# A second mixture's VectorE, ScalarE and transfers in a hand-written order, and an earlier reload of x

## The chip, the cores and the metric

One core of one Trainium2 chip runs the kernel. The metric is the device time of one execution in microseconds; lower is better.

## The reference

Packed attention feeds a mixture of four experts (the first mixture), whose output feeds a second block with a tanh-shrink (called the second mixture here):

```python
p_packed = sm_attn(p, k, v)                  # B=4, H=8, S=576, D=64, 32 packed rows
x = sm_attn(q, p_packed, p_packed)           # -> x, 2304 x 512
for e in range(4):                           # first mixture, 512 -> 1024 -> 512
    out += prob[:, e:e+1] * (np.maximum(x @ w1[e], 0.0) @ w2[e])
h = out @ w_in                               # second mixture, 512 -> 2048
g = h - np.tanh(h)
result = g @ w_out                           # 2048 -> 512
```

All is float32.

## The kernel before

TensorE multiplies float32 in two parts, a high part that its fast format holds and the rest as a low part, and three products (high x high, high x low, low x high) stand for one. ScalarE writes the high part, VectorE subtracts it for the low part.

**First mixture.** Its last chunk ends with the products of L629 (w2) and those of L579. Its results are stored in DRAM and loaded again (`reload`, L643 to L650, one DMA of 256 KB for each 128 tokens, tile `x2`, name x in the trace) for the second mixture; `x_quad` (L685 on) transposes the first six of them on TensorE (L696, tile xps). The order of this part is a list of tokens, one list for each turn: `LASTA` and `LAST` are the last two, `l06` is the reload of tiles 0 to 5, and `q0` to `q3` are `x_quad`. SyncE issues all DMAs, in the order of these lists.

**Second mixture.** The tokens go in NU = 3 units of 768, the 2048 columns in NG = 8 groups of 256: 24 blocks n, block n being group n % 8 of unit n // 8. A block's 768 x 512 by 512 x 256 is done as seven products of quarter size, whose operands are four quarters of x (B11 to B22; B12 only enters differences) and four differences of them (T1 to T4). Each is six matmuls of 128x384 (L795) into one of two PSUM banks (tile h3ps, called X and Z here). The bank is copied out or summed into h: `keep` is a copy on ScalarE (L804), `add` a sum on VectorE (L808), and there are four copies k0 to k3 and three sums a0 to a2 for a block. Products, copies and sums of one block go X0 k0 Z0 a0, X1 k1 Z1 k2, X2 a1 Z2 a2, X3 k3.

The elementwise work on a block is done for its two halves A and B (`elem`, L974, with L985 to L994). h - tanh(h) is taken from tanh where |h| is large and from a polynomial where it is small, so one half is five ScalarE and five VectorE operations on 128x768: ScalarE makes z (square, L985), the mask gh (L986), y in two steps (L987, L988) and t (tanh, L989), VectorE y from z (L990), t (h - tanh, L991), h (L992, L993) and the choice by the mask (L994, `copy_predicated`). `elem_split` then writes the high part (L1006, ScalarE, gh) and the low part (L1012, VectorE, gl). `s4` (L1029) multiplies g by w_out in six tiles of 128 tokens and two halves (ff 0 and 1), three matmuls of 128x512 each, and sums over the unit's eight groups in six PSUM banks (ops). After a unit's last group `s4` evacuates the banks, by turns on VectorE (L1041) and ScalarE (L1039), and stores them.

TensorE's order is written out by hand (`manual_schedule`). In slot n it is X0 Z0, four tiles of block n-2 in ff 0, X1 Z1, four more (two of each ff), X2 Z2, two, X3, two. In slots n = 1 and 9, 10 the next unit's x is transposed too (`x_raw`, L734, tile xps from the pool of six banks), and in slots 3 to 7 and 11 to 15 `x_prep` makes the differences and the parts of it, one step in each slot.

VectorE, ScalarE and SyncE are ordered by the scheduler here, by its own times, with `high_priority(offset=PRIO)` on the copies, sums, transposes' copies and evacuations, and `issue_after` that ties `x_prep` to the sums and copies of block n-1. Weights come by DMA: `load_g` (L771, tile wg, 1.8 MB for a block) and `load_o` (wo, two of 512 KB).

Names of the tables below: h3ps, ops and xps are PSUM banks, gh, gl high and low parts, xr a transposed quarter of x, po an evacuated output tile.

Of the kernel before, what the change touches and what calls it, by code (L numbers as in the profile page):

```python
# [27 lines left out]
PREP = (0, 3, 11)  # L28

# [29 lines left out]
    "d614 _ g7100 _ d615 _ g7101 _ d616 _ g7102 _ d617 g7103 _ d618 "  # L59
# [8 lines left out]
    "w0 l06 g7110 _ d710 _ q0 g7111 _ d711 _ g7112 _ q1 d712 g7113 q2 d713 q3 d714 l69 s0 d715 s1 d716 s2 d717 s3 d718 "  # L68
# [4 lines left out]
def kernel(  # L73
# [647 lines left out]

    def x_raw(u, q, k):
# [21 lines left out]
    def x_prep(u, k):  # L744

        if k == 0:
            x_tiles(u)
            x_split(u, "B11")
            xr["T1"] = xr["B11"]
            x_minus("T1", "B12", "B11")  # L750
        elif k == 1:
            x_split(u, "T1")
            x_split(u, "B22")
        elif k == 2:
            xr["T2"], xr["T3"] = xr["T1"], xr["B12"]
            x_minus("T2", "B22", "T1")
            x_minus("T3", "B22", "B12")
            x_split(u, "T2")
        elif k == 3:
            x_split(u, "B21")  # L760
            xr["T4"] = xr["B22"]
            x_minus("T4", "B21", "T2")
        else:
            x_split(u, "T4")
            x_split(u, "T3")

    wg, xz, hs, late_h, summed, copied = {}, {}, {}, {}, {}, {}
# [5 lines left out]
    def s3(n, step):  # L773


        x = xc[n // NG]
        if step == 0:
            if n == 0:
                xz[n] = [
                    pl.tile([128, 2, 512], F32, tag=tg, name="h3ps")[:, 0, 0:HT]  # L780
                    for pl, tg in ((ps2, "p2"), (psw[0], "pw"))
                ]
                hs[n] = [[u2t([128, HT], F32, "h3") for _ in range(2)] for _ in range(2)]
            else:
                xz[n] = [late["xz"].tile([128, 512], F32, tag="xz", name="h3ps")[:, 0:HT] for _ in range(2)]
                t = late_h[n] = [late["hh"].tile([128, 2, HT], F32, tag="hh", name="h3") for _ in range(2)]
                hs[n] = [[t[k][:, 0], t[k][:, 1]] for k in range(2)]
        X, Z = xz[n]
        (c11, c12), (c21, c22) = hs[n]

        def mul(ps, slot, c, start, stop):
            k = 0
            for kk in range(2):
                for a, b in ((0, 0), (0, 1), (1, 0)):
                    nc.tensor.matmul(  # L795
                        out=ps, lhsT=wg[n][:, a, slot, 128 * kk:128 * kk + 128],
                        rhs=x[c][b][kk] if isinstance(x[c][b], list) else x[c][b][:, kk],
                        start=(start and k == 0), stop=(stop and k == 5), skip_group_check=True,
                    )
                    k += 1  # L800

        def keep(t, ps):
            with tc.high_priority(offset=PRIO):
                copied[n] = nc.scalar.activation(out=t, in_=ps, func=ACTF.Copy).ins  # L804

        def add(t, ps):
            with tc.high_priority(offset=PRIO):
                summed[n] = nc.vector.tensor_tensor(out=t, in0=ps, in1=t, op=ALU.add).ins  # L808

        if step == 0:  # L810
            mul(X, 0, "B11", True, False)
            keep(c11, X)
            mul(Z, 1, "B21", True, True)
            add(c11, Z)
        elif step == 1:
            mul(X, 4, "T2", False, False)
            keep(c12, X)
            mul(Z, 3, "T1", True, False)
            keep(c22, Z)
        elif step == 2:  # L820
            mul(X, 5, "T3", False, False)
            add(c22, X)
            mul(Z, 6, "B22", False, True)
            add(c12, Z)
        else:
            mul(X, 2, "T4", False, True)
            keep(c21, X)
# [146 lines left out]
    def elem(n, fb):  # L974
# [3 lines left out]
        h = hs[n][fb]  # L978
        if n:
            parts = [(slice(None), late_h[n][fb])]  # L980
        else:
            parts = [(k, h[k]) for k in range(2)]
        for k, hk in parts:
            zk, tk, yk, mk = (x if isinstance(k, slice) else x[:, k] for x in (z, t, y, hi))
# [11 lines left out]
    def elem_split(n, fb):  # L996
# [3 lines left out]
        if n:  # L1000
            g = late_h[n][fb].rearrange("p a b -> p (a b)")
            parts = [(0, 2 * HT, g)]
        else:
            parts = [(HT * k, HT * k + HT, hs[n][fb][k]) for k in range(2)]
        for a, b, g in parts:
            nc.scalar.activation(out=hi[:, a:b], in_=g, func=ACTF.Copy)  # L1006
# [9 lines left out]

    ops = {}

    def s4(n, ts, ff):
        u, i = divmod(n, NG)  # L1020
        for t in ts:
# [12 lines left out]
            if i == NG - 1 and ff == 1:  # L1034
                r0 = 768 * u + 128 * t
                o = u2t([128, 512], F32, "po")
                with tc.high_priority(offset=PRIO):
                    if t % 2:
                        nc.scalar.activation(out=o, in_=ps, func=ACTF.Copy)  # L1039
                    else:  # L1040
                        nc.vector.tensor_copy(out=o, in_=ps)  # L1041
                nc.sync.dma_start(out=out[r0:r0 + 128, :], in_=o)
# [4 lines left out]
    for n in range(1, N2 + 2):  # L1047
        if n + 1 < N2:
            load_g(n + 1)
        if n - 1 < N2:  # L1050
            load_o(n - 1)
        order = [[("s", n, k)] if n < N2 else [] for k in range(4)]
        m = n - 2
        if m >= 0:
            order[0].append(("o", m, range(0, 4), 0))
            order[1] += [("o", m, range(4, 6), 0), ("o", m, range(0, 2), 1)]
            order[2].append(("o", m, range(2, 4), 1))
            order[3].append(("o", m, range(4, 6), 1))
# [74 lines left out]
```

## Time and profile before

| | us |
|---|---|
| median of three runs | 1095.16 (1094.71 to 1099.7) |
| profiled execution, its own time | 1096.69 |
| span of its trace | 1094.8 |
| mean granted clock of TensorE | 0.994 |
| TensorE busy | 1068.6 (98%) |
| VectorE, ScalarE busy | 870.3, 619.7 |
| second mixture, X0 of block 2 to X0 of block 24 | 717.07 to 1072.32 |

The span goes from the first to the last instruction. Since TensorE is busy nearly throughout, its own timeline, with the idle time before an instruction and what ended it in square brackets, is the view to read; the queues of the others are read where it waits.

### The profile page before, as it was taken

What the parts mean: (1) busy time and instruction counts of PE and PEld (TensorE: products, weight loads), DVE (VectorE), ACT (ScalarE), POOL (GpSimd) and SP (SyncE); (2) the same over time, 40 slices, a digit from 0 to 9 for tenths busy, and PEclk for the clock granted to TensorE, in tenths of its full rate; (3) what the DMA queues carried; (4) which work ended last, traced back from release to release, by engine and by line L of the source; (5) the groups of instructions that cost most, each with busy time, mean ns of one, the idle gap of its engine ahead of it and who ended that gap; (6) DMA issues with size and microseconds to landing.
All of it is one profiled execution on the core that took longest, in us unless ns stands there. A gap on an engine that the chain in (4) does not pass through costs nothing.

```text
span 1094.8 us, 16535 instructions
## 1 busy us (share of the span) xinstructions
PE 1068.6 (98%) x6356; PEld 904.2 (83%) x6356; DVE 870.3 (79%) x1331; ACT 619.7 (57%) x987; POOL 198.9 (18%) x153
## 2 busy tenths in 40 slices
PE   8899999999999999999999998999999999999998
PEld 6677887888788788888888887888888888989886
DVE  4667879988889775798889864879988888888876
ACT  3345454555554446445454432677786777777674
POOL 0100225544535102243324210000000000000000
PEclk9899999999999999999999999999999999999999
DMA  9616446547436653554364404454555554556432
GB/s 351 209 29 252 154 155 220 182 140 280 175 118 213 241 174 102 178 202 165 118 229 148 169 39 144 161 221 148 202 193 170 205 186 156 206 196 217 174 134 87
DMA packets 57582, 192.74 MB, mean 176 GB/s; under 512 B 6432, under 2 KB 8480, under 8 KB 54432
## 3 DMA queue, kind: packets, MB, share of 16 engines
q1 hardware_dynamic: 57504, 191.69, 50.1%
q8 instruction: 50, 0.82, 0.3%
q14 instruction: 28, 0.23, 0.1%
HBM read 144.74 MB, written 46.92 MB: 175 GB/s over the span
## 4 chain that ended last, share of the span: by engine, by line
PE 78%; DVE 11%; ACT 7%; issue 2%; DMA 1%; POOL 0%; SPq 0%; DVEq 0%; ACTq 0%
PE yps L629 31%; PE ops L1029 13%; PE h3ps L795 12%; PE hpx L579 7%; PE hpz L579 6%; PE wps L484 3%; PE hps L531 2%; PE pv L256 1%; ACT z L985 1%; ACT t L989 1%; DVE h L994 1%; DVE h L993 1%; ACT gh L986 1%; DVE y L990 1%; DMA x<-xs 1%
## 5 line engine op out<-in xcount | busy, mean ns | idle before, releaser
L1029 PE MATMUL ops<-wo,gh 128*128 128x512 f32 x576 | 179.0, 392 | 0.7 <-ACT gh L1006 0.7
L640 DVE SCALAR_TENSOR_TENSOR x<-yps,pn,x 128x512 f32<-128x512 f32 x126 | 93.9, 745 | 47.9 <-PE yps L629 47.7
L1029 PEld LDWEIGHTS ops<-wo,gh 128*128 128x128 f32 x576 | 106.7, 188 | 19.4 <-ACT gh L1006 1.1
L629 PE MATMUL yps<-w2h,h0h 128*128 128x512 f32 x288 | 117.5, 408 | 2.6 <-DVE a2l L324 1.4
L1029 PE MATMUL ops<-wo,gl 128*128 128x512 f32 x288 | 113.7, 395 | 0.9 <-DVE gl L1012 0.9
L629 PE MATMUL yps<-w2h,h0l 128*128 128x512 f32 x288 | 113.6, 394 | 0.0
L629 PE MATMUL yps<-w2h,h1h 128*128 128x512 f32 x288 | 113.2, 393 | 0.0
L629 PE MATMUL yps<-w2l,h0h 128*128 128x512 f32 x288 | 113.0, 392 | 0.0
L629 PE MATMUL yps<-w2h,h1l 128*128 128x512 f32 x288 | 112.6, 391 | 0.0
L629 PE MATMUL yps<-w2l,h1h 128*128 128x512 f32 x288 | 112.5, 391 | 0.0
L795 PE MATMUL h3ps<-xh,wg 128*128 128x384 f32 x384 | 107.4, 339 | 1.8 <-ACT h L804 1.6
L629 PEld LDWEIGHTS yps<-w2h,h0h 128*128 128x128 f32 x288 | 54.1, 188 | 34.5 <-issue 21.8
L579 PE MATMUL hpx<-th,wp 128*128 128x288 f32 x336 | 81.8, 299 | 0.6 <-ACT p L586 0.5
L1006 ACT ACTIVATE gh<-h 128x768 fp32r<-128x768 f32 (+1 forms) x50 | 41.0, 819 | 67.5 <-DVE h L994 67.5
L377 POOL TENSOR_TENSOR fo<-fo,f 128x512 f32<-128x512 f32 x32 | 44.0, 1377 | 179.2 <-DVE f L373 97.7
L795 PEld LDWEIGHTS h3ps<-xh,wg 128*128 128x128 f32 x384 | 70.3, 188 | 6.0 <-ACT h L804 3.7
L471 POOL TENSOR_TENSOR w2l<-wraw,w2h 128x512 fp32r<-128x512 f32 x32 | 43.1, 1368 | 147.4 <-ACT w2h L469 145.6
L991 DVE TENSOR_TENSOR t<-h,t 128x768 f32<-128x768 f32 (+1 forms) x50 | 46.1, 923 | 26.4 <-ACT t L989 26.4
L795 PE MATMUL h3ps<-xl,wg 128*128 128x384 f32 x192 | 64.6, 337 | 0.2 <-DVE xl L150 0.2
L795 PE MATMUL h3ps<-xbh,wg 128*128 128x384 f32 x224 | 63.2, 339 | 1.6 <-ACT h L804 1.1
L1029 PEld LDWEIGHTS ops<-wo,gl 128*128 128x128 f32 x288 | 54.0, 187 | 12.8 <-DVE gl L1012 1.3
L629 PEld LDWEIGHTS yps<-w2l,h1h 128*128 128x128 f32 x288 | 54.4, 189 | 12.1
(177 smaller groups left out, 2634.7 us busy)
## 6 DMA issues: line engine op xcount, KB each, us to landing
wg<-wing SPq DMA_DIRECT2D x24, 1792.0 KB, 7.4
wraw<-in_w_dram SPq DMA_DIRECT2D x48, 512.0 KB, 5.6
wo<-wout SPq DMA_DIRECT2D x48, 512.0 KB, 5.4
w2s<-w2h SPq DMA_DIRECT2D x16, 512.0 KB, 7.1
w2s<-w2l SPq DMA_DIRECT2D x16, 512.0 KB, 7.4
f<-in_win_dram SPq DMA_DIRECT2D x16, 512.0 KB, 7.1
f<-in_wout_dram SPq DMA_DIRECT2D x16, 512.0 KB, 6.6
wing<-f SPq DMA_DIRECT2D x32, 256.0 KB, 4.3
```

The source lines that it names most:

```text
L256: nc.tensor.matmul(out=pv[64 * h:64 * h + 64, jj, :], lhsT=kv_v[b][c][0:n, 128 * j + 64 * h:128 * j + 64 * h + 64], rhs=a1t[:, c, k0:k0 + ...
L377: nc.gpsimd.tensor_tensor(out=lf, in0=lf, in1=st[:, :, 1].bitcast(F32), op=ALU.mult)
L471: nc.gpsimd.tensor_tensor(out=l[:, k], in0=r[:, k], in1=f(h[:, k]), op=ALU.subtract)
L484: nc.tensor.matmul(out=ps[32 * j:32 * j + 32, r, :], lhsT=ppbd[p][d, bi, j, 32 * r:32 * r + 32], rhs=raw[0, c, j // 2][d, j % 2, :],)
L531: nc.tensor.matmul(out=ps[:, ff, 0:n], lhsT=a[c, p, bi][:, g, c0:c0 + 128], rhs=x[p][:, g, t0:t0 + n], start=(k == 0), stop=(k == 5),)
L579: nc.tensor.matmul(out=ps[:, ff, 0:HB], lhsT=W[a][:, slot, c0], rhs=x[b], start=(start and k == 0), stop=(stop and k == 2), skip_group_che ...
L629: nc.tensor.matmul(out=ps, lhsT=a[:, ff, o:o + 128], rhs=w[c, fp][:, ff], start=(k == 0), stop=(k == 11),)
L640: last[0] = nc.vector.scalar_tensor_tensor(out=x2[tt], in0=ps, scalar=pn[:, tt, e:e + 1], in1=x2[tt], op0=ALU.mult, op1=ALU.add,).ins
L795: nc.tensor.matmul(out=ps, lhsT=wg[n][:, a, slot, 128 * kk:128 * kk + 128], rhs=x[c][b][kk] if isinstance(x[c][b], list) else x[c][b][:, k ...
L991: nc.vector.tensor_tensor(out=tk, in0=hk, in1=tk, op=ALU.subtract)
L1006: nc.scalar.activation(out=hi[:, a:b], in_=g, func=ACTF.Copy)
L1029: nc.tensor.matmul(out=ps, lhsT=a, rhs=wo[n][ff][:, w], start=(i == 0 and ff == 0 and k == 0), stop=(i == NG - 1 and ff == 1 and k == 2), ...
```

## The change

It does four things.

- The token `l06` moves from the start of `LAST` to the end of `LASTA`, ahead of the weight load of the first block in SyncE's queue.
- Slots n = 2 to 25 are put under `manual_schedule` for SyncE, VectorE and ScalarE as well. One line for each kind of slot says the order: X and Z are products, k and a copies and sums, o tiles of `s4`, v evacuations, R and C transposes and their copies, P, H and D the parts of `x_prep`; a letter with A or B is one elementwise operation on that half (z, t, y, q, m, g on ScalarE, d, c, r, f, p, l on VectorE, l the low part).
- Elementwise work on block n-1 stands in slot n, its last low part in slot n+1, and the tiles of `s4` are those of block n-2 as before.
- Banks X and Z change places from block to block (`xz[n].reverse()`), and of the six copies of x in slot 10 one moves from VectorE to ScalarE.

```diff
+SLOT = (
+    "lB zA tA X0 k0 dA yA Z0 a0 cA P o030 qA mA rA fA zB pA X1 tB k1 dB Z1 k2 cB yB o450 o011 qB rB gA X2 a1 fB mB "
+    "Z2 a2 H pB o231 lA D X3 k3 gB o451 "
+)
...
+SLOT_LAST = (
+    "lB zA tA yA dA cA qA mA rA fA o030 pA zB tB gA lA o450 o011 dB yB cB qB mB rB o231 fB pB o451 gB nB "
+)
+SLOT_OUT = "o050 o001 v0 o111 v1 o221 v2 o331 v3 o441 v4 o551 v5 "
...
 LASTA = (
-    "d614 _ g7100 _ d615 _ g7101 _ d616 _ g7102 _ d617 g7103 _ d618 "
+    "d614 _ g7100 _ d615 _ g7101 _ d616 _ g7102 l06 _ d617 g7103 _ d618 "
 )
...
 LAST = (
-    "w0 l06 g7110 _ d710 _ q0 g7111 _ d711 _ g7112 _ q1 d712 g7113 q2 d713 q3 d714 l69 s0 d715 s1 d716 s2 d717 s3 d718 "
+    "w0 g7110 _ d710 _ q0 g7111 _ d711 _ g7112 _ q1 d712 g7113 q2 d713 q3 d714 l69 s0 d715 s1 d716 s2 d717 s3 d718 "
 )
...
-            if u == 2 and (k == 1 or q == 3):
+            if u == 2 and k == 1:
                 nc.vector.tensor_copy(out=o, in_=ps)
...
+    X_PREP = (
+        ("", "hB11", "lB11 sT1"),
+        ("", "hT1 hB22", "lT1 lB22"),
+        ("sT2 sT3", "hT2 hB21", "lT2"),
+        ("lB21 sT4", "hT4 hT3", ""),
+        ("lT4 lT3", "", ""),
+    )
...
+            if n % 2 == 0:
+                xz[n].reverse()
...
-        for u in (1, 2):
-            if 0 <= n - PREP[u] < 5:
-                with tc.issue_after(summed[n - 1]), tc.issue_after(copied[n - 1]):
-                    x_prep(u, n - PREP[u])
...
+    progs = {
+        NG + 1: SLOT_RAW, NG + 2: SLOT_RAW2, 2 * NG + 1: SLOT_END, 2 * NG + 2: "v5 v4 " + SLOT,
+        N2: SLOT_LAST, N2 + 1: SLOT_OUT,
+    }
+    with tc.manual_schedule(engines=rest):
+        for n in range(2, N2 + 2):
+            slot(n, progs.get(n, SLOT))
```

TensorE's instructions stand in the same order in both programs, and block by block they use the same PSUM banks from n = 2 on. The other engines' rows move. SyncE's queue at the end of the first mixture, before (wout is a store of prepared weights, wg the first blocks' weights, x the reloaded tiles):

```order
L401 DMA wout_133<-fh 128x512
L401 DMA wout_133<-fo 128x512
L771 DMA wg<-wing_110 128x3584
L650 DMA x_6436<-xs_101 128x512
L650 DMA x_6438<-xs_102 128x512
L650 DMA x_6440<-xs_103 128x512
L650 DMA x_6442<-xs_104 128x512
L650 DMA x_6444<-xs_105 128x512
L650 DMA x_6446<-xs_106 128x512
L771 DMA wg<-wing_111 128x3584
```

and now:

```order
L427 DMA wout_133<-fh 128x512
L427 DMA wout_133<-fo 128x512
L676 DMA x_6398<-xs_101 128x512
L676 DMA x_6400<-xs_102 128x512
L676 DMA x_6402<-xs_103 128x512
L676 DMA x_6404<-xs_104 128x512
L676 DMA x_6406<-xs_105 128x512
L676 DMA x_6408<-xs_106 128x512
L815 DMA wg<-wing_110 128x3584
L815 DMA wg<-wing_111 128x3584
```

The six loads of x went ahead of the first block's weights. ScalarE between the last copy of block 17 (k1, h_9112) and the first of block 18 (h_9261), where the second unit's outputs are evacuated, before:

```order
L804 ACTIVATE h_9112<-h3ps 128x384
L985 ACTIVATE z<-h_9111 128x768
L989 ACTIVATE t<-h_9111 128x768
L1039 ACTIVATE po<-ops 128x512 x2
L985 ACTIVATE z<-h_9112 128x768
L989 ACTIVATE t<-h_9112 128x768
L1039 ACTIVATE po<-ops 128x512
L986 ACTIVATE gh<-z,cst 128x768
L987 ACTIVATE y<-z,cst 128x768
L804 ACTIVATE h_9261<-h3ps 128x384
```

and now (h_9083 is block 17, h_9232 block 18; L1077 is the evacuation, L1096 z, L1098 t, L1104 the mask, L1116 the high part):

```order
L1077 ACTIVATE po<-ops 128x512
L1116 ACTIVATE gh<-h_8950 128x768
L1104 ACTIVATE gh<-z,cst 128x768
L1077 ACTIVATE po<-ops 128x512
L857 ACTIVATE h_9083<-h3ps 128x384
L1116 ACTIVATE gh<-h_8951 128x768
L1077 ACTIVATE po<-ops 128x512
L1096 ACTIVATE z<-h_9082 128x768
L1098 ACTIVATE t<-h_9082 128x768
L857 ACTIVATE h_9232<-h3ps 128x384
```

Two of the evacuations moved ahead of block 17's last copy, and of the next block's elementwise work only z and t stand ahead of block 18's first copy. VectorE in slot 9, around the sums of block 9 (h_7955, h_7956) and the first copy of a transposed quarter of x (L740), before:

```order
L1012 TENSOR_TENSOR gl<-h_7823,gh 128x512
L1012 TENSOR_TENSOR gl<-h_7823,gh 128x256
L808 TENSOR_TENSOR h_7956<-h3ps,h_7956 128x384
L994 COPY_PREDICATED h_7824<-gh,t 128x768
L808 TENSOR_TENSOR h_7955<-h3ps,h_7955 128x384
L1012 TENSOR_TENSOR gl<-h_7824,gh 128x256
L1012 TENSOR_TENSOR gl<-h_7824,gh 128x512
L1041 COPY po<-ops 128x512 x2
L991 TENSOR_TENSOR t<-h_7955,t 128x768
L740 COPY xr<-xps 128x384
```

and now (h_7926, h_7927 are block 9; L863 is the sum, L1079 the evacuation, L772 the copy of x, L1044 the low part):

```order
L1110 SCALAR_TENSOR_TENSOR y<-z,y 128x768
L1079 COPY po<-ops 128x512
L863 TENSOR_TENSOR h_7927<-h3ps,h_7927 128x384
L1112 SCALAR_TENSOR_TENSOR h_7795<-y,h_7795 128x768
L863 TENSOR_TENSOR h_7926<-h3ps,h_7926 128x384
L1114 COPY_PREDICATED h_7795<-gh,t 128x768
L1079 COPY po<-ops 128x512
L772 COPY xr<-xps 128x384
L1044 TENSOR_TENSOR gl<-h_7794,gh 128x512
L1044 TENSOR_TENSOR gl<-h_7794,gh 128x256
```

The two evacuations now stand apart, one ahead of the sums and one right ahead of the copy of x, and the low parts behind that copy; the next block's elementwise work no longer stands between.

## Rows read from the trace of the kernel before

**Rows 1.** The page's first part: busy time, share, instructions of each engine.

```profile
PE 1068.6 (98%) x6356; PEld 904.2 (83%) x6356; DVE 870.3 (79%) x1331; ACT 619.7 (57%) x987; POOL 198.9 (18%) x153
```

**Rows 2.** TensorE's timeline, end of first mixture: start, length, instruction, [idle before, releaser].

```profile
664.23 0.39 PE L629 MATMUL yps<-w2h,h1l 128*128 128x512 f32 x1
667.66 0.33 PE L696 MATMUL xps<-ident,x 128*128 128x128 f32 x1 [3.05 <-DMA x<-xs]
...
672.53 0.40 PE L629 MATMUL yps<-w2h,h0h 128*128 128x512 f32 x1
...
675.27 0.29 PE L579 MATMUL hpx<-th,wp 128*128 128x288 f32 x1
...
676.85 0.82 PE L696 MATMUL xps<-ident,x 128*128 128x128 f32 x6
```

**Rows 3.** Windows around it: stretch, length, busy PE, PEld, DVE, ACT, POOL, clock, DMA.

```profile
660.00:664.00 4.00, 4.00 (x24) 3.52 (x23) 1.89 (x3) 1.33 (x2) 0.00 (x0) 1.00 0.94 396
669.00:671.00 2.00, 2.00 (x10) 2.00 (x11) 0.00 (x0) 0.81 (x1) 0.00 (x0) 0.52 0.04 8
```

**Rows 4.** SyncE's timeline ahead of it.

```profile
639.62 0.32 SPq L401 DMA_DIRECT2D wout<-fo  x1
657.54 0.32 SPq L771 DMA_DIRECT2D wg<-wing  x1
657.91 3.23 SPq L650 DMA_DIRECT2D x<-xs  x6
```

**Rows 5.** Windows of slots 2, 9 with 10, 18 and 23.

```profile
717.07:733.63 16.56, 16.03 (x81) 14.16 (x80) 13.45 (x19) 12.27 (x20) 0.00 (x0) 1.00 0.44 152
...
828.86:867.41 38.55, 34.95 (x182) 30.57 (x180) 32.08 (x46) 28.78 (x44) 0.00 (x0) 1.00 0.57 197
...
977.45:994.12 16.67, 15.90 (x79) 14.02 (x78) 13.70 (x19) 13.46 (x21) 0.00 (x0) 1.00 0.77 268
1056.68:1072.32 15.64, 15.64 (x79) 14.10 (x78) 12.65 (x18) 11.31 (x17) 0.00 (x0) 1.00 0.22 67
```

**Rows 6.** TensorE's timeline: transposes of slots 1 and 9, a product of slot 18.

```profile
716.50 0.82 PE L734 MATMUL xps<-ident,x 128*128 128x128 f32 x6
...
844.39 0.87 PE L734 MATMUL xps<-ident,x 128*128 128x128 f32 x6 [2.17 <-DVE po L1041]
...
983.22 0.44 PE L795 MATMUL h3ps<-xh,wg 128*128 128x384 f32 x1 [0.77 <-ACT h L804]
```

**Rows 7.** TensorE's timeline in the tail.

```profile
1081.36 0.74 PE L1029 MATMUL ops<-wo,gh 128*128 128x512 f32 x2 [0.70 <-ACT gh L1006]
...
1082.99 0.50 PE L1029 MATMUL ops<-wo,gl 128*128 128x512 f32 x1 [0.90 <-DVE gl L1012]
```

**Rows 8.** VectorE's timeline in slot 23.

```profile
1059.37 0.96 DVE L991 TENSOR_TENSOR t<-h,t 128x768 f32<-128x768 f32 x1 [1.55 <-ACT t L989]
...
1060.71 0.95 DVE L992 SCALAR_TENSOR_TENSOR h<-z,h 128x768 f32<-128x768 f32 x1
1061.58 0.95 DVE L990 SCALAR_TENSOR_TENSOR y<-z,y 128x768 f32<-128x768 f32 x1
...
1064.14 0.96 DVE L990 SCALAR_TENSOR_TENSOR y<-z,y 128x768 f32<-128x768 f32 x1 [0.62 <-ACT y L988]
```

**Rows 9.** VectorE by form, 860 to 1090: count | busy, mean ns | idle before.

```profile
L994 DVE COPY_PREDICATED h<-gh,t 128x768 f32<-128x768 uint32 x28 | 30.1, 1074 | 0.3
L993 DVE SCALAR_TENSOR_TENSOR h<-y,h 128x768 f32<-128x768 f32 x28 | 26.7, 953 | 0.5
L808 DVE TENSOR_TENSOR h<-h3ps,h 128x384 f32<-128x384 f32 x41 | 21.8, 548 | 2.7 <-PE h3ps L795 2.2 <-ACT h L804 0.6
L1012 DVE TENSOR_TENSOR gl<-h,gh 128x512 fp32r<-128x512 f32 x29 | 19.8, 683 | 0.0
L1012 DVE TENSOR_TENSOR gl<-h,gh 128x256 fp32r<-128x256 f32 x28 | 11.7, 420 | 1.6 <-ACT gh L1006 1.6
```

**Rows 10.** ScalarE's timeline in slot 18, an operation on 128x768.

```profile
979.07 0.85 ACT L985 ACTIVATE z<-h 128x768 f32<-128x768 f32 x1
```

More of the change, by code (lines that the diff above doesn't have):

```diff
@@ L771, in load_g @@
         nc.sync.dma_start(out=f(wg[n]).rearrange("p l s f -> p l (s f)"), in_=wing[n % NG])
-    def s3(n, step):
[L776 to L783, printed above, removed]
-            else:
[L785 to L827, printed above, removed]
@@ new lines, with product @@
+    PRODUCTS = {
+        "X0": (0, "B11", True, False), "Z0": (1, "B21", True, True), "X1": (4, "T2", False, False),
+        "Z1": (3, "T1", True, False), "X2": (5, "T3", False, False), "Z2": (6, "B22", False, True),
+        "X3": (2, "T4", False, True),
+    }
+    def product(n, name):
+        if name == "X0":
+            s3_begin(n)
+        x, ps = xc[n // NG], xz[n]["XZ".index(name[0])]
+        slot, c, start, stop = PRODUCTS[name]
+        k = 0
+        for kk in range(2):
+            for a, b in ((0, 0), (0, 1), (1, 0)):
+                nc.tensor.matmul(
+                    out=ps, lhsT=wg[n][:, a, slot, 128 * kk:128 * kk + 128],
+                    rhs=x[c][b][kk] if isinstance(x[c][b], list) else x[c][b][:, kk],
+                    start=(start and k == 0), stop=(stop and k == 5), skip_group_check=True,
+                )
+                k += 1
@@ new lines, in keep, with add @@
+    def keep(n, k):
+        i, (a, b) = "XXZX"[k], ((0, 0), (0, 1), (1, 1), (1, 0))[k]
+        with tc.high_priority(offset=PRIO):
+            nc.scalar.activation(out=hs[n][a][b], in_=xz[n]["XZ".index(i)], func=ACTF.Copy)
+    def add(n, k):
+        i, (a, b) = "ZXZ"[k], ((0, 0), (1, 1), (0, 1))[k]
+        t = hs[n][a][b]
+        with tc.high_priority(offset=PRIO):
+            nc.vector.tensor_tensor(out=t, in0=xz[n]["XZ".index(i)], in1=t, op=ALU.add)
+    def s3(n, step):
+        for op in ("X0 k0 Z0 a0", "X1 k1 Z1 k2", "X2 a1 Z2 a2", "X3 k3")[step].split():
+            if op[0] in "XZ":
+                product(n, op)
+            else:
+                {"k": keep, "a": add}[op[0]](n, int(op[1]))
@@ L1015, in elem_split, with s4 @@
                     )
+    def elem_split(n, fb):
+        parts = [(HT * k, HT * k + HT, hs[n][fb][k]) for k in range(2)]
+        for a, b, g in parts:
+            nc.scalar.activation(out=gh[n][fb][:, a:b], in_=g, func=ACTF.Copy)
+        low_part(n, fb, parts)
     ops = {}
-    def s4(n, ts, ff):
+    def s4(n, t0, t1, ff):
         u, i = divmod(n, NG)
-        for t in ts:
+        for t in range(t0, t1 + 1):
             if i == 0 and ff == 0:
@@ L1033, in s4 @@
                 )
[L1034 to L1042, printed above, removed]
-    load_g(1)
-    for fb in range(2):
-        elem(0, fb)
@@ L1047, with evacuate, el_tiles @@
-    for n in range(1, N2 + 2):
+    def evacuate(n, t):
+        r0 = 768 * (n // NG) + 128 * t
+        o = u2t([128, 512], F32, "po")
+        if t % 2:
+            nc.scalar.activation(out=o, in_=ops[n // NG, t], func=ACTF.Copy)
+        else:
+            nc.vector.tensor_copy(out=o, in_=ops[n // NG, t])
+        nc.sync.dma_start(out=out[r0:r0 + 128, :], in_=o)
+    el = {}
+    def el_tiles(n, fb):
+        for k in "zty":
+            el[k, fb] = late["el"].tile([128, 2, HT], F32, tag=k, name=k)
+        hi = late["gh"].tile([128, 2, HT], F32R, tag="gh", name="gh")
+        gh.setdefault(n, []).append(hi.rearrange("p a b -> p (a b)"))
@@ L1048, with slot @@
+    def slot(n, prog):
         if n + 1 < N2:
```

185 lines of the change are left out of this document (118 added, 67 removed).

## The prediction

> **What bounds the kernel now.** The page's first part comes first: TensorE is busy in 98% of the span, 1068.6 of 1094.8 us [rows 1]. So nothing is won by making another engine's work shorter; a change wins only where TensorE stands still, or runs at a lower clock, because somebody is late. I looked for these places along TensorE's own timeline.
>
> The first is the end of the first mixture, where x is loaded again. A product of L629 starts at 664.23, and the transposes of the reloaded x start at 667.66 after 3.05 us of waiting for the DMA [rows 2]. The granted clock was 1.00 in the 4 us before and 0.52 in 2 us behind the pause, that is nearly all at the lower of its two levels, 1.2 GHz in place of 2.4 [rows 3], so the products of L579 behind the transposes ran at half pace. SyncE's queue tells why x is late: its last store was issued at 639.62, then the queue stood in front of a weight load for 18 us, until 657.54, and the six x loads stand behind it [rows 4].
>
> The second is the second mixture. Its work goes in slots of one block each; a slot in which TensorE waits for nothing takes 15.64 us, and there VectorE is busy for 12.65 and ScalarE for 11.31 [rows 5]. The slots n=2 to 23 run from 717.07 to 1072.32 = 355.25 us. Their floor is 22 x 15.64 = 344.08, plus the 24 transposes of slots 9 and 10, six of which take 717.07 - 716.50 = 0.57 [rows 5, 6]: 4 x 0.57 = 2.28. So **8.89 us** are waits. They are uneven: 0.92 in n=2, 38.55 - 31.28 - 2.28 = 4.99 in n=9 and 10, 1.03 in n=18, and 1.95, the rest, in five others of 0.1 to 0.5. What TensorE waits for there is a PSUM bank or an operand that ScalarE or VectorE could have had ready: a transpose stands 2.17 us for an output evacuation that VectorE had put late, and the first product after a unit's end 0.77 us for a copy of ScalarE that stood behind two evacuations [rows 6]. Both engines have 3 to 4 us to spare per slot; it is their order that is late.
>
> The third is the tail: two waits of 0.70 and 0.90 us for the last block's elementwise result [rows 7].
>
> **The change part by part.**
>
> *Reload.* The x loads move in SyncE's queue from behind the weight load to ahead of it. The queue is free for them after 639.62 + 0.32 = 639.94; the six issues took 3.23 us, to 657.91 + 3.23 = 661.14 [rows 4], and by 672.53 all that needs x on TensorE was over [rows 2], so the last load took at most 11.4 us. Issued by 643.2, x is there by 654.6, ten us early; nearly twice that time would still be hidden. The weight load behind them waits until 657.54 for TensorE to leave its buffer, which the six loads don't touch, so to stand behind them costs it nothing, and the next weight load comes 3 us sooner. What is won: twelve products take 675.27 - 672.53 = 2.74, 0.228 each, so the next thing after 664.23 could start at 664.46. Transposes and twelve L579 products need 0.57 + (676.85 - 675.27 = 1.58) = 2.15 at full clock; they took 672.53 - 664.46 = 8.07 [rows 2, 6]. The gain is **5.9 us**. If the clock dipped all the same, only the wait would go, 3.05 and two of about 0.3: 3.6. I take 5.9, since the clock was 1.00 until TensorE stopped [rows 3].
>
> *Order of the second mixture.* TensorE's rows are the same in both programs, and so is the turn of its two PSUM banks from n=2 on: "banks by turns" costs and brings nothing. The arithmetic is the same too, except that one 128x384 copy goes from VectorE to ScalarE. What changes is the place of everything on VectorE and ScalarE. Elementwise work is put one step behind the products, the copies and sums that free a bank stand where the product ends, and evacuations of a finished unit stand between. In a slot ScalarE has two operations, z and t, ahead of the first copy; in slot 18 one evacuation stands ahead of these two, where before three evacuations, with z and t of both halves, m and y, stood between the last copy of one block and the first of the next. The sum of each slot's work is unchanged, so the question is whether each engine can keep the new order in 15.64 us. VectorE is the fuller one. Its independent operations start 0.87 apart (1060.71, 1061.58), though one is listed with 0.95 [rows 8]. In slots 3 to 7 and 11 to 15 the next unit's x is split as well, two to three more such operations: 12.65 + 3 x 0.87 = 15.3 of 15.64. That fits, by little, and the products that wait for VectorE's sums have about 1 us of margin by a walk through the order. Slots 9 and 10 take 1.14 more because of the transposes, and there I find every copy ahead of its transpose, but two products of slot 10 with next to none to spare; I leave 0.4 there. So the gain is 8.9 - 0.4 = **8.5**. Its ends: nothing excludes a loss (rivals below); above, 8.9 is all there is.
>
> Weighed against that: the rows of the form list 0.953 us for such an operation, 0.683 and 0.420 for the two sizes of the low parts, 0.548 for a sum, 1.074 for the predicated copy [rows 9]. The Trainium skill (VectorE: DVE Perf Modes, section The DRAIN you can't avoid) says that the next VectorE operation does not start until the pipe of the one before has emptied, with an exception for one that is not held. By that rule a slot's operations would be added up at their full listed durations, and the prep slots would not fit. The starts 0.87 apart are what the exception says, not the rule. What the rule would give is the third rival.
>
> *Tail.* With ops at listed length, the last block's second half is ready after two ScalarE ops (1.7), five of VectorE (4.8), one of ScalarE (0.85), the low parts (1.1), five more (4.8) and the last ScalarE op (0.85) = 14.1 us; TensorE comes to it after 18 tiles of three products, 54 x 0.228 = 12.3 [rows 2, 9, 10]. A wait of 1.8 in place of 0.70 + 0.90 = 1.60 [rows 7]: -0.2. With starts 0.87 apart the ten VectorE ops take 0.9 less: +0.7. I take **+0.2**: the order that cures both small waits puts the first half's low parts in front of the second half.
>
> *Sum.* 5.9 + 8.5 + 0.2 = 14.6. The profiled execution took 1096.69 (span 1094.8), which would be 1082.1; it is 1.53 above the median of the runs, so the forecast is 1095.16 - 14.6 = **1080.6 us**.
>
> **The rivals.**
>
> *The unit ends stay late.* Slots 9, 10 and 18 hold 4.99 + 1.03 = 6.0 of the 8.89. There evacuations, transposes' copies, splits and elementwise work all meet, and my margins are thinnest. For it: VectorE was busy for 32.08 of 38.55 us in slots 9 and 10 already [rows 5]. Against it: the waits were of single misplaced ops. Half kept gives 1083.2 or so, all of it 1086.2.
>
> *The reload's place is taken by another wait*, such as operands of the products behind the transposes, which nobody had to deliver before 669: nothing won there, 1080.6 + 5.9 = 1086.5. Against it: between the last transposes and 676.85 the timeline shows no wait of TensorE, at either clock.
>
> *VectorE is full in the prep slots.* At listed durations a slot's VectorE work is 2 x (4 x 0.953 + 1.074) + 3 x 0.548 + 2 x (0.683 + 0.420) = 13.6 [rows 9]; two or three more make 15.5 and 16.5. With one wait for ScalarE as in the trace, 1.55 [rows 8], that is 17.1 and 18.0, or 1.4 over the floor in eight slots and 2.4 in two: 16 us, and the whole gain is given back with a little more: 1096.6. Against it: the starts 0.87 apart. The rule cited from the Trainium skill above would bring this about.
>
> *Slower: a loop of ScalarE and VectorE in the fixed order.* ScalarE's last op of a slot (g of half B) stands ahead of the next z and t of half A, these ahead of VectorE's d of A, and VectorE then runs through both halves to the p that g needs. At listed lengths the loop is 3 x 0.85 + 10 ops (9.77) + three sums (1.64) = 13.96 [rows 9, 10]. It decides above 15.64, since TensorE's waits then follow it slot by slot, at 2.2 us for each 0.1. A scheduler can fill a gap with the next op that is ready; a fixed order can't. With both of the waits that the steady slot showed, 1.55 and 0.62 [rows 8], it is 16.13: 22 x 0.49 = 10.8, and two more ops in six of the prep slots inside it, 6 x 1.9 = 11.4. That is 22.2 over the floor instead of 8.9, less the reload's 5.9: 7.4 us slower than before, 1102.6. Against it: those waits are results of the old order, and about 2 us of slack is left without them.
>
> **How the numbers follow.** Forecast 0.64 (1078 to 1084), unit ends 0.12, reload 0.08, VectorE full 0.08, loop 0.08. The range goes from 1077.8 (tail at its best end and the 0.4 of slot 10 as well, and a little more elsewhere) to 1088.0, which takes in the first two rivals and leaves out 0.16 and the forecast's thin edges. A measurement of this kernel can tell about 0.5%, 5.5 us: faster 0.64 + 0.12 + 0.08 = 0.84, same 0.08 (VectorE full), slower 0.08 (loop).
>
> **What would show it.** Reload: x issues at 640 and no pause and no lower clock around 664; products of L629 again 2.2 us after it. Order: X0 starts 15.64 apart in n=2 to 23, and 16.8 in 9 and 10. A VectorE chain without gaps in slots 5 and 13 with TensorE waiting for a sum would show the third rival; gaps on both VectorE and ScalarE by turns with slots above 15.64 everywhere, the loop. I am wrong if the slots without prep are longer than 15.64, if a wait stands in front of the products that follow the transposes, or if the tail's one wait is over 3 us.

## The result, and the profile after

| | before | changed |
|---|---|---|
| median, us | 1094.93 (1093.8 to 1099.7, 4 runs) | 1081.4 (1080.2 to 1082.05, 4 runs) |
| profiled execution, its own time | 1096.69 | 1081.32 |
| its span | 1094.8 | 1079.5 |
| its X0 of block 2 to the start of slot 24 | 355.25 | 346.87 |

(There is no block 24: what the table of the kernel before calls X0 of block 24 is the first instruction of slot 24, a tile of `s4`.)

The ratio is 0.9867, with a 95% interval of 0.9837 to 0.9897, which is 14.6 us of the time before; the two medians are 13.5 us apart. 14.6 were forecast, and the median of 1081.4 lies 0.8 above the forecast time. The page's first part says that TensorE is as full as before and the others no emptier:

```profile
PE 1062.6 (98%) x6356; PEld 903.7 (84%) x6356; DVE 872.5 (81%) x1330; ACT 626.5 (58%) x988; POOL 199.0 (18%) x153
```

So the gain is to be read from TensorE's timeline. At the reload (start, length, instruction), where [rows 2] had 3.05 us of waiting:

```profile
663.31 0.39 PE L655 MATMUL yps<-w2h,h1l 128*128 128x512 f32 x1
663.54 0.82 PE L722 MATMUL xps<-ident,x 128*128 128x128 f32 x6
664.11 0.38 PE L605 MATMUL hpx<-th,wp 128*128 128x288 f32 x1
...
665.79 0.39 PE L655 MATMUL yps<-w2h,h0h 128*128 128x512 f32 x1
```

No bracket stands behind any of them, and 665.79 is 2.25 us behind 663.54, where it was 8.07. SyncE's timeline has the reason, six issues 17.5 us ahead of the weight load that had held them up [rows 4]:

```profile
638.70 0.32 SPq L427 DMA_DIRECT2D wout<-fo  x1
639.07 2.82 SPq L676 DMA_DIRECT2D x<-xs  x6
656.62 18.20 SPq L815 DMA_DIRECT2D wg<-wing  x2
```

The windows answer to [rows 3, 5] (stretch, length, busy PE, PEld, DVE, ACT, POOL, clock, DMA share, GB/s; the stretch behind the transposes, then slots 2, 9 with 10, and 23):

```profile
665.00:667.00 2.00, 2.00 (x14) 1.79 (x13) 0.00 (x0) 1.51 (x3) 0.00 (x0) 1.00 0.00 0
710.28:726.04 15.76, 15.76 (x81) 14.18 (x80) 12.48 (x17) 11.68 (x19) 0.00 (x0) 1.00 0.54 195
819.88:853.81 33.93, 33.93 (x182) 30.73 (x180) 29.96 (x43) 27.37 (x42) 0.00 (x0) 1.00 0.62 225
...
1041.51:1057.15 15.64, 15.64 (x79) 14.10 (x78) 12.76 (x17) 11.46 (x18) 0.00 (x0) 1.00 0.20 67
```

The clock is 1.00 where it was 0.52. In each window TensorE is busy for the whole of it, and slots 9 and 10 take 33.93 us instead of 38.55. From slot 2 to 23 the starts of X0 are 15.64 to 15.66 apart, but for slot 2 (15.76) and slots 9 and 10 (16.88, 17.04). One wait is left, in the tail [rows 7]:

```profile
1071.39 0.73 PE L1067 MATMUL ops<-wo,gh 128*128 128x512 f32 x2 [1.83 <-ACT gh L1116]
```

**By stages, from the two traces.** From the start of the last product group ahead of the transposes (661.68 and 660.77) to X0 of block 2 (717.07 and 710.28): 55.39 before, 49.51 now, **5.88** less. From there to the start of slot 24 (1072.32 and 1057.15): **8.38** less. From there to the end of TensorE's last product (1090.99 and 1075.78): 18.67 and 18.63, **0.04** less. That makes 14.3. TensorE's last product ended 15.21 us earlier; the remaining 0.9 is the difference of 661.68 and 660.77, up to where TensorE has the same work in both programs. 0.7 of it is there already behind the first stage (last section), which the change does not touch.

### The profile page after: what moved, and what is told of

Read it like the earlier page. It is cut to its first block, busy times and chain, and to the rows that moved or that the text cites. A ratio compares the mean times of both kernels' runs of the same rounds, so it can differ in the third digit from the quotient of the medians.

```text
span 1079.5 us, 16546 instructions
## 1 busy us (share of the span) xinstructions
PE 1062.6 (98%) x6356; PEld 903.7 (84%) x6356; DVE 872.5 (81%) x1330; ACT 626.5 (58%) x988; POOL 199.0 (18%) x153
## 4 chain that ended last, share of the span: by engine, by line
PE 86%; DVE 9%; ACT 3%; issue 1%; DMA 0%; POOL 0%; SPq 0%; DVEq 0%; ACTq 0%
PE yps L655 31%; PE ops L1067 17%; PE h3ps L847 16%; PE hpx L605 7%; PE hpz L605 5%; PE wps L510 3%; PE hps L557 2%; PE qsc L304 1%; PE pv L282 1%; DVE x L666 1%; PE sc L226 1%; DVE h0l L542 1%; DVE h1l L542 1%; DVE wp L534 1%; DMA f<-in_wout_dram 0%
## 5 line engine op out<-in xcount | busy, mean ns | idle before, releaser
L857 ACT ACTIVATE h<-h3ps 128x384 f32<-128x384 f32 x96 | 46.9, 490 | 74.7 <-PE h3ps L847 72.3
L655 PEld LDWEIGHTS yps<-w2h,h0l 128*128 128x128 f32 x288 | 54.0, 188 | 12.1
L655 PEld LDWEIGHTS yps<-w2h,h1l 128*128 128x128 f32 x288 | 54.1, 188 | 12.0
L655 PEld LDWEIGHTS yps<-w2h,h1h 128*128 128x128 f32 x288 | 54.1, 188 | 11.6
```

Source lines behind the costliest of these rows:

```text
L655: nc.tensor.matmul(out=ps, lhsT=a[:, ff, o:o + 128], rhs=w[c, fp][:, ff], start=(k == 0), stop=(k == 11),)
L857: nc.scalar.activation(out=hs[n][a][b], in_=xz[n]["XZ".index(i)], func=ACTF.Copy)
```

## The experiments

Stages are given as above: reload (55.39 before, 49.51 changed), slots (355.25 and 346.87; the floor, 22 slots of 15.64 and the transposes' 2.28, is 346.36) and tail (18.67 and 18.63). They are used because whole times carry the first stage's scatter (last section). They come from one trace of each version.

**The reload alone**, in the kernel before:

```diff
 LASTA = (
-    "d614 _ g7100 _ d615 _ g7101 _ d616 _ g7102 _ d617 g7103 _ d618 "
+    "d614 _ g7100 _ d615 _ g7101 _ d616 _ g7102 l06 _ d617 g7103 _ d618 "
...
-    "w0 l06 g7110 _ d710 _ q0 g7111 _ d711 _ g7112 _ q1 d712 g7113 q2 d713 q3 d714 l69 s0 d715 s1 d716 s2 d717 s3 d718 "
+    "w0 g7110 _ d710 _ q0 g7111 _ d711 _ g7112 _ q1 d712 g7113 q2 d713 q3 d714 l69 s0 d715 s1 d716 s2 d717 s3 d718 "
```

> The kernel before with the reload of x issued ahead of the weight load, nothing else. My theory: the pause of 3.05 us and the half-pace stretch behind it go together, so TensorE comes from the last product ahead of the transposes to the first behind them in 2.2 us instead of 8.1, and the whole is 5.8 us shorter (about 1089); the second mixture's slots keep their 8.9 us over the floor. Rival A, the clock dips all the same: 3.6 shorter, and the granted clock is again near 0.5 in a stretch of 2 us there. Rival B, the gain is only to be had with the new order, since the scheduler moves the waits: the second mixture's excess grows and the whole is less than 4 shorter.

Measured: 0.9916 of before (0.9899 to 0.9932). In its trace reload 49.52, slots 355.21, tail 18.67. The stretch behind the transposes and slots 9 and 10:

```profile
666.00:668.00 2.00, 2.00 (x13) 1.79 (x13) 0.00 (x0) 1.46 (x3) 0.00 (x0) 1.00 0.00 0
823.01:861.56 38.55, 34.96 (x181) 30.60 (x180) 32.08 (x46) 28.79 (x44) 0.00 (x0) 1.00 0.57 197
```

The reload gives its 5.87 with the clock at 1.00, and the slots keep every wait, 38.55 us to the hundredth. Rivals A and B fall. (The ratio alone would say 9 us, the stages say 5.9. The traced execution is the longest of the four. On record beside each time is its mean granted clock: 0.995 for the traced one and 0.998 to 1.000 for the other three, 0.993 to 0.998 for those of the kernel before. The last section has what goes with that; the untraced executions themselves can't be taken apart into stages.)

**The order alone**: the changed kernel with `l06` back at the start of `LAST`.

> The changed kernel with the reload put back behind the weight load. My theory: the two parts add, so this is 8.4 us shorter than before (about 1086.5) and 5.8 longer than the changed kernel; slots 2 to 23 have at most 0.6 us over the floor, and the pause of 3 us with the low clock behind it is back. Rival, the parts share a cause (an early reload relieves the DMA queue for the slots): the slots' excess comes back in part, over 2 us.

Measured: 0.9925 of before (0.9905 to 0.9944). Reload 55.36, slots 346.85: by the stages the two parts add, and neither touches the other's stage. (The whole times can't show it: the two ratios, 9 and 8 us, make more than the 14.6 of both together.) The pause is back with its low clock. What was not expected is the tail, 20.22 instead of 18.63. The wait there is the same, but the windows behind it show a clock that fell to 0.50:

```profile
1075.41 0.73 PE L1067 MATMUL ops<-wo,gh 128*128 128x512 f32 x2 [1.81 <-ACT gh L1116]
```

```profile
1075.00:1077.00 2.00, 1.59 (x6) 1.26 (x7) 1.61 (x3) 0.35 (x1) 0.00 (x0) 0.88 0.00 0
1077.00:1079.00 2.00, 2.00 (x6) 1.52 (x6) 0.37 (x2) 0.60 (x1) 0.00 (x0) 0.50 0.38 149
1079.00:1081.00 2.00, 2.00 (x8) 1.60 (x7) 0.68 (x2) 0.60 (x1) 0.00 (x0) 0.77 0.63 245
```

**Which engine's order carries the gain.** ScalarE alone by hand, VectorE left to the scheduler (and the mirror image, with `Activation` taken out), the evacuations with the priority that they had before:

```diff
-    with tc.manual_schedule(engines=rest):
+    with tc.manual_schedule(engines=rest - {mybir.EngineType.DVE}):
...
+        with tc.high_priority(offset=PRIO):
+            if t % 2:
```

> The changed kernel with only ScalarE and SyncE in the hand-written order of the second mixture; VectorE's is left to the scheduler, with its priority for evacuations as before. My theory: the old waits were single misplaced operations, most of them on ScalarE (0.92 in slot 2, 1.95 in five, 1.03 in slot 18, about 1.1 in slot 10), so slots 2 to 23 have 0.5 to 3 us over the floor of 346.4, not 8.9. Rival (only the two orders together work, since each engine's order is laid out for the other's): over 5 us.

> The other half: VectorE and SyncE in the hand-written order, ScalarE left to the scheduler. My theory: the ScalarE waits of before come back, slots 2 to 23 have 4 to 6 us over the floor and TensorE's waits there end with ScalarE. Rival, as for the other half: over 8 us, since VectorE's fixed order can't give way to a late ScalarE; or, if VectorE's order carried the gain, under 1.

ScalarE by hand: slots 347.78, 1.42 over the floor, as expected; the time of its one run is 1077.69. Its tail is 17.68, 0.95 shorter than that of the changed kernel, whose slots are 0.91 shorter: from the last product group ahead of the reload to TensorE's end both take **415.0** us. So in these traces ScalarE's order, with SyncE's, brings the whole gain of the hand-written order, and writing out VectorE's by hand as well moved 0.9 us from the slots to the tail and won nothing. VectorE by hand: slots **367.51**, 21.15 over the floor and 12.3 more than before, and a tail of 22.27; 1103.07. I had expected 4 to 6 over the floor, and the rival (over 8, since VectorE's fixed order can't give way to a late ScalarE) is what came. A quarter of the 21.15, 5.39, is slot 10, where TensorE waits once for 3.19 us and the clock falls behind it:

```profile
846.01 0.44 PE L847 MATMUL h3ps<-xbh,wg 128*128 128x384 f32 x1 [3.19 <-ACT h L857]
```

A slot without any preparation of x, in the trace of VectorE by hand, as a window and on ScalarE and VectorE:

```profile
1025.48:1041.81 16.33, 16.16 (x80) 13.92 (x79) 12.66 (x18) 11.09 (x18) 0.00 (x0) 1.00 0.44 171
```

```profile
1024.29 0.49 ACT L857 ACTIVATE h<-h3ps 128x384 f32<-128x384 f32 x1 [3.68 <-PE h3ps L847]
1024.67 0.84 ACT L1097 ACTIVATE z<-h 128x768 f32<-128x768 f32 x1
1025.41 0.84 ACT L1099 ACTIVATE t<-h 128x768 f32<-128x768 f32 x1
1026.14 0.83 ACT L1097 ACTIVATE z<-h 128x768 f32<-128x768 f32 x1
1026.88 0.83 ACT L1117 ACTIVATE gh<-h 128x768 fp32r<-128x768 f32 x1
...
1030.00 0.47 ACT L857 ACTIVATE h<-h3ps 128x384 f32<-128x384 f32 x1
...
1032.02 1.76 ACT L1103 ACTIVATE y<-y,cst 128x768 f32<-128x768 f32 x2
...
1036.08 0.85 ACT L1117 ACTIVATE gh<-h 128x768 fp32r<-128x768 f32 x1 [1.56 <-DVE h L1115]
1040.61 0.49 ACT L857 ACTIVATE h<-h3ps 128x384 f32<-128x384 f32 x1 [3.69 <-PE h3ps L847]
```

```profile
1027.74 1.03 DVE L1044 TENSOR_TENSOR gl<-h,gh 128x256 fp32r<-128x256 f32 x2 [1.64 <-ACT gh L1117]
...
1030.50 0.56 DVE L863 TENSOR_TENSOR h<-h3ps,h 128x384 f32<-128x384 f32 x1 [0.87 <-ACT h L857]
...
1032.98 0.96 DVE L1111 SCALAR_TENSOR_TENSOR y<-z,y 128x768 f32<-128x768 f32 x1 [1.06 <-ACT y L1103]
```

Both engines have time to spare (12.66 and 11.09 of 16.33), and the slot is 0.69 over the floor all the same. ScalarE takes g of half B (1026.88) behind z and t of half A and z of half B, the first copy (1030.00) behind y and m, and the second step of y (1032.02) behind y and m of half B; VectorE stands for each of them, 1.64 + 0.87 + 1.06 = 3.57 us, and ScalarE then stands for 3.69 at k3 with its queue behind it. While the kernel runs, both engines work through fixed lists; the scheduler can give way only while it writes its list, by its own times. Here the list that it wrote for VectorE went well with ScalarE's hand-written one, and the list that it wrote for ScalarE did not go with VectorE's. This second list is neither ScalarE's old order nor the hand-written one, so the old waits, which the expectation wanted back, were not what was tried; and with one list of each kind it is not shown that the same holds for others.

**Is it order or occupancy?** More work, of the same kind, at places of my choice, in slots 19 to 23. First VectorE, with y of a finished half minus itself, three (and later five) between the two low parts:

```diff
+            elif op == "x":
+                y = el["y", int(arg)].rearrange("p a b -> p (a b)")
+                nc.vector.tensor_tensor(out=y, in0=y, in1=y, op=ALU.subtract)
...
-            slot(n, progs.get(n, SLOT))
+            p = progs.get(n, SLOT)
+            slot(n, p.replace("lA D", "lA x0 x1 x0 D") if 19 <= n < N2 else p)
```

> The changed kernel with three more VectorE operations on 128x768 in each of slots 19 to 23, between the low parts of half A and those of half B, where VectorE waits for ScalarE; they write a dead tile. My theory (independent operations start 0.87 apart): 2.6 us more in a slot whose trace shows 2.7 us of VectorE gaps, so the slots stay at 15.64 and nothing is lost. Rival (each operation waits for the one before to empty, listed lengths add up): 13.6 + 2.9 = 16.5 in a slot, 0.85 over, so 2 to 4 us longer over the five slots. If it were the length of VectorE's work and not its order that made the old waits, this would lose them again.

> The changed kernel with five more VectorE operations on 128x768 in each of slots 19 to 23, where three cost no slot anything; they write dead tiles. The trace of the changed kernel has 2.7 us of VectorE gaps in a slot. My theory (independent operations start 0.87 apart): 4.35 us more fill the gaps and 1.6 over, so slots grow to about 17.3 once the slack of the first is gone, 4 to 7 us in the five, and VectorE shows no gap of its own. Rival (listed lengths add up): 13.6 + 4.8 = 18.4, 2.75 over, 10 us or more.

With three more, slots 346.86: nothing lost, though VectorE was busy for 15.07 of a slot. The tail took 19.63, one more, since the last extra operations stand at the head of the last block's chain, and there nothing hides them; "nothing is lost" was wrong in this place. With five more, slots 21 to 23 take 16.91 each, 3.83 us together (19 and 20 live on slack), a little under the 17.3 and the 4 to 7 us that were expected; the tail grew to 22.68. VectorE's timeline has no bracket in such a slot. Slot 22 with three more, slot 22 with five more, and VectorE in the latter:

```profile
1024.41:1040.06 15.65, 15.65 (x80) 14.10 (x79) 15.07 (x21) 11.45 (x18) 0.00 (x0) 1.00 0.53 206
```

```profile
1025.92:1042.84 16.92, 15.91 (x80) 14.04 (x78) 16.75 (x24) 11.54 (x17) 0.00 (x0) 1.00 0.49 191
```

```profile
1026.25 4.42 DVE L1148 TENSOR_TENSOR y<-y 128x768 f32<-128x768 f32 x5
1030.59 1.02 DVE L1044 TENSOR_TENSOR gl<-h,gh 128x256 fp32r<-128x256 f32 x2
```

Five operations take 1030.59 - 1026.25 = 4.34 us, 0.87 each. A VectorE without a gap needs 16.91, so its own work of a slot is 16.91 - 4.34 = 12.57 us, not the 13.6 of the listed lengths. Added at full length, five more would have cost 2.75 a slot; they cost 1.27. The Trainium skill (VectorE: DVE Perf Modes, section The DRAIN you can't avoid) has the rule that the next operation does not start until the pipe of the one before is empty, and the exception that "a next op that is not held starts earlier". This trace agrees with the exception: 0.87 from start to start where 0.95 is listed.

Then ScalarE: four copies of dead tiles onto themselves, once ahead of z and t, once ahead of the copy k3.

```diff
-            slot(n, progs.get(n, SLOT))
+            p = progs.get(n, SLOT)
+            slot(n, p.replace("lB zA", "lB x0 x1 x0 x1 zA") if 19 <= n < N2 else p)
```

(the second with `"D X3"` and `"D x0 x1 x0 x1 X3"`).

> The changed kernel with four more ScalarE operations on 128x768 at the head of each of slots 19 to 23, between g of half B and the next z; they copy dead tiles onto themselves. They start 0.73 apart: 2.9 us more. By occupancy alone ScalarE has 4.3 us to spare, so nothing would be lost. By the loop (g, z, t on ScalarE, then VectorE through both halves to the p that g needs): VectorE's later gaps of 0.77 and 0.55 take up 1.3, the wait of g for its place behind k3 another 1.0, and 0.6 us a slot is left over, which adds up from slot to slot; TensorE's first wait is in slot 20, for a sum or a copy, and the five slots lose 2 to 3.5 us together.

> The same four ScalarE operations a slot, in slots 19 to 23, as in the run that put them ahead of z and lost 2.5 us there, now in ScalarE's gap of 3.4 us ahead of the copy k3; they copy dead tiles onto themselves. By the loop theory this place is outside it: 2.9 us fit into 3.4, the slots stay at 15.64 and the tail as it was. Rival (any four more operations of ScalarE cost, because it is nearer to full than its busy time says): slots at 16 or more again.

First ahead of z, then ahead of k3, slot 22 of each:

```profile
1025.63:1041.78 16.15, 15.95 (x79) 13.97 (x78) 12.59 (x19) 14.27 (x21) 0.00 (x0) 1.00 0.51 202
```

```profile
1026.97:1042.61 15.64, 15.64 (x79) 14.10 (x78) 12.76 (x17) 14.38 (x22) 0.00 (x0) 1.00 0.56 213
```

ScalarE is as busy in the one as in the other, 14.3 us, and the one loses 2.47 us in the five slots, the other none (slots 346.85, tail 18.61). The tail of the first, not forecast, took 20.56, with a wait of 2.12 us and the clock at 0.50 behind it. In the first TensorE's X1 waits for k0, and VectorE waits 3.38 us for t, here in slot 22:

```profile
1030.83 0.44 PE L847 MATMUL h3ps<-xh,wg 128*128 128x384 f32 x1 [0.20 <-ACT h L857]
```

```profile
1030.44 0.96 DVE L1106 TENSOR_TENSOR t<-h,t 128x768 f32<-128x768 f32 x1 [3.38 <-ACT t L1098]
```

The slot settles at 16.15, so the loop of g, z, t and VectorE's way to p is 16.15 - 4 x 0.73 = 13.2 us without the additions, 2.4 under the 15.64 of a slot. (An estimate: it takes the loop for the only thing that sets 16.15. In that trace ScalarE is never idle from g of half B, 1025.16, through t, nor VectorE from there through p, and the next g starts at 1041.30.) (Whether TensorE's wait would be for a copy or a sum the expectation left open.)

**Banks by turns.** The changed kernel without `xz[n].reverse()`.

> The changed kernel without the line that lets the two product banks change places. My theory: the banks come out the same for every product, so this is the changed kernel once more: about 1081.4, slots at 15.64, a tail wait of 1.8 with or without a dip of the clock behind it. Rival (the turns matter): X0 of a slot waits for the copy k3 on ScalarE instead of a sum, and slots grow by 0.2 or more.

Measured: 1080.39 (1079.55 to 1081.01, 4 runs), 0.9877 of before (0.986 to 0.9893). Slots 346.86, tail 18.59: the changed kernel once more. In the programs as built X and Z of every block have the same two banks with the line and without it, and in the kernel before: the banks change places anyway.

**The tail.** z and t of the last block's half A before k3, and VectorE's low parts to places where it waits. On ScalarE the high part of half A (gA) also goes behind two more operations of half B:

```diff
 SLOT_LAST = (
-    "lB zA tA yA dA cA qA mA rA fA o030 pA zB tB gA lA o450 o011 dB yB cB qB mB rB o231 fB pB o451 gB nB "
+    "yA dA cA lB qA mA rA fA o030 pA zB tB dB yB cB qB rB gA lA o450 o011 fB mB o231 pB o451 gB nB "
 )
...
+            elif op == "e":
+                el_op(n, arg[0], "AB".index(arg[1]))
...
+            slot(n, p.replace("X3 k3", "X3 ezA etA k3") if n == N2 - 1 else p)
```

> The changed kernel with the last block's elementwise chain begun earlier: z and t of its half A stand on ScalarE in slot 23 ahead of the last copy k3, and in slot 24 the low parts go to places where VectorE waits. My theory (the tail's one wait of 1.83 is the length of that chain and of the low parts in it): about 2 us of the chain go, so the wait falls to 0.3 or less and TensorE's last stretch, from X0 of slot 24 to its end, from 18.6 to 16.8. A dip of the clock behind that wait, which cost 1.6 in some runs, can't come either. 1.8 to 3 us shorter than the changed kernel: about 1079. Rival: the wait is set by the products behind the last evacuations or by k3 being later, and stays over 1 us.

Measured: **1077.05** (1075.21 to 1078.05, 5 runs), 0.9842 of before (0.9825 to 0.9859), 3.3 below the kernel without turns, which ran beside it: a little more than the 1.8 to 3 expected. The traces give 2.1 of it to the tail, 16.49 instead of 18.63 (18.59 without turns); where the rest of the medians' difference comes from they don't show. The page's group of these products, changed kernel and then this one (count | busy, mean ns | idle before):

```profile
L1067 PE MATMUL ops<-wo,gh 128*128 128x512 f32 x576 | 178.9, 391 | 1.8 <-ACT gh L1116 1.8
```

```profile
L1067 PE MATMUL ops<-wo,gh 128*128 128x512 f32 x576 | 178.7, 391 | 0.0
```

and ScalarE's timeline of this one, where z starts 1.5 us ahead of k3 and the last g is ready at 1067.6:

```profile
1053.26 0.85 ACT L1096 ACTIVATE z<-h 128x768 f32<-128x768 f32 x1 [1.90 <-DVE h L863]
1054.01 0.83 ACT L1098 ACTIVATE t<-h 128x768 f32<-128x768 f32 x1
1054.81 0.49 ACT L857 ACTIVATE h<-h3ps 128x384 f32<-128x384 f32 x1
...
1066.71 0.85 ACT L1116 ACTIVATE gh<-h 128x768 fp32r<-128x768 f32 x1 [3.23 <-DVE h L1114]
```

This is the best of the versions that were timed in rounds: TensorE has no wait of 0.2 us or more left from the reload to its end. Which of the moves brings how much was not tried. ScalarE by hand, whose scheduled VectorE takes the low part of half A between the operations on half B but whose z and t start no earlier, had a tail of 17.68.

## Why the prediction was right, point by point

- *Reload*, 5.9: 5.88 in the changed kernel, 5.87 with the reload alone. The x loads landed before they were needed, the weight load behind them lost nothing (656.62 is as far ahead of the product at 660.77 as 657.54 was of that at 661.68), and the choice of 5.9 over 3.6 (the clock stays up if TensorE doesn't stop) is shown by the window at 1.00.
- *Order*, 8.5: 8.38. Of the 0.4 left for slot 10 it took 0.26 (17.04 against 16.78), without a listed wait; slots 2 and 9 kept 0.1 each. That the waits were of order and not of occupancy is shown by the order alone, which takes them away with the same work, and by the pair on ScalarE: the same busy time, 2.47 us or none by place alone. The step that prices VectorE by starts 0.87 apart is shown by the run with five more operations. (The first reading of slot 18 counts two evacuations ahead of the copy; the later one, three, is what the order list shows.)
- What the prediction did not see: the two orders are not of equal weight. ScalarE's alone brings the slots to 1.4 over the floor and, with its shorter tail, the same 415.0 us; VectorE's alone makes the slots 12.3 us longer than before.
- *Tail*, +0.2: 0.04. The wait is 1.83 where the working at listed lengths gave 1.8, and the value taken lay between that and the one for starts 0.87 apart: a compromise whose reason was not the one that held. VectorE's timeline shows why the listed lengths were the better price here; the five operations on half A:

```profile
1058.69 0.96 DVE L1106 TENSOR_TENSOR t<-h,t 128x768 f32<-128x768 f32 x1 [0.44 <-ACT t L1098]
1059.68 0.96 DVE L1108 SCALAR_TENSOR_TENSOR h<-z,h 128x768 f32<-128x768 f32 x1
1060.56 0.95 DVE L1110 SCALAR_TENSOR_TENSOR y<-z,y 128x768 f32<-128x768 f32 x1
1061.54 0.96 DVE L1112 SCALAR_TENSOR_TENSOR h<-y,h 128x768 f32<-128x768 f32 x1
1062.60 1.08 DVE L1114 COPY_PREDICATED h<-gh,t 128x768 f32<-128x768 uint32 x1
```

  The five take 1062.60 + 1.08 - 1058.69 = 4.99 us, no less than their lengths together. Three of them start 0.98 to 1.06 behind the one before: the second overwrites the h that the first reads, the fourth needs the y of the third, the fifth the h of the fourth. Only the third, which needs nothing of the second, starts 0.88 behind it.
- *Banks by turns*, nothing: shown.
- *The sum*, 14.6: 14.3 by stages, 13.5 by the medians, 14.6 by the ratio. The whole times alone, which scatter by some us, could not have told such sums apart; that the parts came out is shown by the stages.
- *Rivals.* Unit ends and reload: out, by the windows of slots 9, 10 and the reload. VectorE full: out, but by less than a slot's 12.57 us of work says. In slots 5 and 13, where VectorE has most to do, the first half of its sign came: its timeline has no bracket there, and it is busy for 15.47 of 15.64 us, where the prediction had 15.3. The second half, TensorE waiting for a sum, did not. Slot 5 of the changed kernel:

```profile
757.32:772.96 15.64, 15.64 (x79) 14.09 (x78) 15.47 (x21) 13.02 (x21) 0.00 (x0) 1.00 0.53 191
```

  The slower case did not come in the changed kernel, whose loop is 13.2 us where the rival had 13.96 at listed lengths. Where VectorE's order was fixed and ScalarE's was not, the time was 1103.07, near the rival's 1102.6, but that is in part luck. The slots are 21.15 over the floor (22.2 forecast) by other parts: the forecast spread them over all slots, with 0.49 in each and 1.9 more in six of the prep slots, and the trace has 5.39 in slot 10 and 0.7 in each of the last five. The tail is 3.6 longer, which the rival did not have, and the first stage of this one execution is about 4 shorter. The mechanism is related, two in-order lists that wait for each other by turns; the loop itself is another, since ScalarE's order there is the scheduler's.

## What to carry to other kernels

When the bounding engine waits though the others have a quarter of their time to spare, look for the single operations that stand in front of the ones it waits for, and price a new order by the gaps and loops of one period, not by busy time: here four operations cost 2.5 us at one place of a queue and nothing at another. Before all engines get a fixed order, try it on one: here ScalarE's alone, the engine that VectorE waits for in the middle of its chain, brought all of the order's gain, and VectorE's alone lost 12.3 us in the slots. A load that waits for nothing belongs ahead of one that waits in the same queue, and what it wins can be more than the wait, here 5.9 us for 3.6 of waiting, because the clock stayed up.

## What the runs showed of the hardware

At the tail's wait the granted clock fell in some executions and not in others. It fell to 0.50, the lower of the two levels, with waits of 1.81, 2.12, 2.35 and 2.69 us (order alone; four more ScalarE operations ahead of z; five more on VectorE; VectorE by hand), which cost 1.6 us more in the first, and it stayed at 1.00 with 1.83, 1.80 and 1.81 (changed kernel, without turns, four in the gap) and 2.08 us (three more on VectorE). In slot 10 of the kernel before it stayed at 1.00 behind a wait of 2.17 [rows 6]. So the length of the wait alone does not decide: 1.81 us stands on both sides. What does is not settled by these runs. Where no wait of the tail was over 0.90 us (before, reload alone, ScalarE by hand, the chain begun earlier) there was no fall before TensorE's last product.

The scatter of the whole time has its place in the first 63 us of the kernel, the attention stage, where the same instructions of TensorE took from 59.4 to 64.0 us in the twelve profiled executions; the 597 us from there to the end of the first mixture agree within about 0.7 us. That is why stages are compared here and not whole times. The length of that stage goes with TensorE's granted clock in it. The windows of the first 63 us, ScalarE by hand and then the kernel before:

```profile
0.00:63.00 63.00, 56.49 (x587) 43.56 (x587) 35.07 (x87) 25.78 (x52) 7.51 (x13) 1.00 0.71 243
0.00:63.00 63.00, 56.86 (x561) 43.78 (x562) 33.32 (x82) 23.73 (x47) 7.49 (x13) 0.92 0.70 243
```

The two executions with a clock of 1.00 there come to the last product group ahead of the reload's transposes at 657.1 and 657.4; the three with 0.97 at 659.0; the three with 0.95 at 659.3 to 659.6; and the four with 0.92, the kernel before and the changed one among them, at 660.8 to 661.9. Why the clock fell more often in one execution than in another was not tried.
